# An attention and feed-forward kernel: step 3's Y transposed by DMA, the inclusive decay sums of steps 6 and 7 made by VectorE, and a new order from step 3 on

## The chip, the cores and the metric

The kernel runs on one core of one Trainium2 chip. The metric is the time of one launch on the device, in microseconds (us); lower is better. Several runs of the kernel are given by their median.

## What is computed

A linear attention with a decaying state (RWKV-6) runs over 4 sequences of 768 tokens with 8 heads of 48 channels. Its output is the input of a feed-forward layer with squared ReLU. The reference, cut to what matters:

```python
# r, k, v, w: (4, 8, 768, 48); u: (8, 48)
state = zeros((B, H, D, D))
for t in range(S):
    cur = einsum('bhd,bhe->bhde', u * k[t], v[t])
    y[t] = einsum('bhd,bhde->bhe', r[t], state + cur)
    state = w[t][..., None] * state + einsum('bhd,bhe->bhde', k[t], v[t])
# y as x: (3072, 384); w_in: (384, 2048); w_out: (2048, 384)
h = x @ w_in
out = square(maximum(h, 0)) @ w_out
```

## The kernel before

**Tiling.** The 3072 tokens are cut into 12 steps of 256 tokens, three steps for each of the four sequences. Each step has two halves of 128 tokens. A step goes through two parts. In the attention part the products of neighbouring decays are made (`ww_`), their logarithms (`lw_`), and TensorE sums those over the tokens with triangular matrices (`cum_`, lines 336 to 340): an exclusive sum, and an inclusive one with the sign turned. ScalarE takes the exponentials of both (`exp_`, `ac_`). r and k are multiplied by these decays (`rd_`), the results transposed (`tr_` and `rkt_` on TensorE and a copy, or `dtr_` by DMA), TensorE forms the products of r and k inside a chunk (`p_`, line 408), VectorE masks them (`pm_`), and the state is carried on by `su_` (TensorE, line 430), `ts_` (a sum) and `sn_` (a product on GpSimd). The output Y is collected in PSUM by `y_`, `yc_` and `yq_` (line 454); `yq_` adds the share of a token's own key through `ku_`, `qp_`, `q_` and `vq_`. `ysb_` copies Y to SBUF.

**From Y to the feed-forward part.** Y has to be transposed for the next product. `yt_` does it with six TensorE transposes into PSUM (line 500), and `xt_` copies them to SBUF. `dyt_` does it with one DMA transpose from SBUF to SBUF, issued by SP (line 507). Before, steps 0 to 3 take `yt_` and `xt_`, steps 4 to 11 take `dyt_`.

**The inclusive sum.** If a step has a word `ni_`, `cum_` leaves out its last matrix product (line 340) and VectorE makes the inclusive sum from the exclusive one and the logarithms (`ni_`, line 348). Before, steps 8 to 11 do so.

**The feed-forward part.** `m1_` makes the first product in eight groups per step (line 517, six matrix products each), `rl_` applies the ReLU (ScalarE, line 524, or VectorE, line 526), `sq_` squares (lines 532 and 534), and the second product follows as `m2_` (line 540) for steps 0 to 4. Steps 5 to 11 use Strassen's scheme in Winograd's form for it, with seven products of half size (`pw_`, line 594), sums of inputs (`sw_`, line 572, on VectorE or GpSimd) and of outputs (`cx_`, `ow_`). `store` writes the result.

**The order.** One string, `ORDER`, holds every operation of the program as a word: its name, its step, further numbers, after a colon the PSUM bank, after an equals sign the engine (A ScalarE, V VectorE, G GpSimd). The loop at the end of the kernel issues the words one after the other. Each engine therefore works through its own words in the order in which they stand in the string, and waits at a word until its inputs are there and its target is free. Loads, stores, `dtr_` and `dyt_` all go through SP's one queue in the same way. Buffers are handed out in the order of the words.

```python
    def dyt_(s):
        nc.sync.dma_start_transpose(
            out=buf("xT", s)[:].rearrange("p c a t -> p (c a) t"),
            in_=buf("y_sb", s)[:].rearrange("p c d -> p (c d)"))
    ...
        nc.tensor.matmul(cs[:, 0, 0:DM], tri_strict[:], lw[:, :, 0:D], start=True, stop=True)
        if s not in by_vector:
            nc.tensor.matmul(cs[:, 1, 0:DM], tri_incl_neg[:], lw[:, :, 0:D], start=True, stop=True)

    by_vector = {int(word.partition("=")[0].split(".")[1]) for word in ORDER.split() if word.startswith("ni_.")}
```

Of the kernel before, what the change touches and what calls it, by code (L numbers as in the profile page):

```python
# [50 lines left out]
sq_.4.1=A vq_.7 yc_.6 dtr_.7.0 yq_.6 m1_.5.4:3 ysb_.6=V lw_.8 rl_.5.5=A m1_.5.0:2 kw_.8=G ts_.7.0=V rl_.5.4=A dyt_.6
cum_.8:1 rl_.5.0=V m2_.4.1.0:0 ku_.8 ac_.8 sq_.5.3=A ni_.8=V m2_.4.0.0:1 store.3.1 rw_.8=V m1_.5.3:2 ld.8.v exp_.8
ld.9.k ww_.9=G m2_.4.0.1 sq_.5.2=A rd_.8.1 m2_.4.0.2 ld.9.r rl_.5.3=A sn_.7.0 m2_.4.0.3 rd_.8.0 ld.10.w sq_.5.1=A
m2_.4.1.1 qp_.8 ts_.7.1=V m2_.4.1.2 sq_.5.0=A p_.7.1:0 p_.7.0:1 store.3.0 os_.4.0=A pm_.7.1 sn_.7.1 m1_.6.7:2
store.0.1 m1_.6.2:3 sw_.5.1.1=G rl_.6.7=A pm_.7.0 m1_.6.6:1 rl_.6.2=A m1_.6.1:2 v_.8=A sw_.5.0.1=V sw_.5.0.2=V y_.7:1
rl_.6.6=A tw_.2=V su_.8:0 lw_.9 yc_.7 yq_.7 kw_.9=V m1_.6.3:3 ysb_.7=A rw_.9=V m1_.6.4:1 rl_.6.1=A sw_.5.0.3=V dyt_.7
sw_.5.1.3=V cum_.9:1 rl_.6.4=A ww_.10=V m2_.4.1.3 sw_.5.1.2=V rl_.6.3=A dtr_.8.0 m1_.6.5:2 ni_.9=V sq_.6.1=A tw_.4=V
pw_.5.2:1 dtr_.8.1 os_.4.1=A pw_.5.1:3 sw_.5.1.4=G exp_.9 m1_.6.0:0 cx_.5.1=V ac_.9 store.1.1 rl_.6.5=V pw_.5.6
sw_.5.0.4=G rl_.6.0=A ld.10.k rd_.9.1 m1_.7.7:2 sq_.6.0=A ld.9.v ku_.9 ow_.5.1=V m1_.7.5:0 ld.11.w rd_.9.0 rl_.7.7=A
pw_.5.5 cx_.5.2=A rl_.7.5=A ts_.8.0=V dtr_.9.0 m1_.7.4:2 lw_.10 cx_.5.3=V sn_.8.0 q_.8 p_.8.0:0 rl_.7.4=A p_.8.1:1  # L60
m1_.7.1:0 sq_.6.2=A pm_.8.0 vq_.8 pw_.5.7 rl_.7.1=A pm_.8.1 pw_.5.3 sq_.6.3=A dtr_.9.1 ku_.10 m1_.7.3:2 ow_.5.2=V
v_.9=A ow_.5.4=V m1_.7.0:0 sw_.6.1.1=V rl_.7.3=A y_.8:0 rl_.7.0=A sw_.6.1.2=V su_.9:1 sw_.6.0.1=V sq_.7.2=A yc_.8
sw_.6.0.2=V yq_.8 sw_.6.1.3=V pw_.5.4 ysb_.8=A sw_.6.0.3=V ww_.11=V m1_.7.6:1 ts_.9.0=A dyt_.8 ow_.5.3=V pw_.6.1:2
sn_.9.0 rl_.7.6=A m1_.7.2:0 sq_.7.3=A qp_.9 store.5.1 ts_.9.1=V pw_.6.2:1 ld.10.r rl_.7.2=V cx_.6.1=A lw_.11 ld.11.r
p_.9.1:0 p_.9.0:1 sq_.7.1=A ld.11.k pw_.6.6 sw_.6.1.4=G pm_.9.0 store.5.0 m1_.8.4:3 ld.10.v kw_.10=G q_.9 m1_.8.7:0
rl_.8.4=A store.4.1 cum_.10:1 cx_.6.2=A sw_.6.0.4=G ow_.6.1=V m1_.8.1:3 rl_.8.7=A ni_.10=V pw_.6.5 pm_.9.1 exp_.10
rw_.10=G pw_.6.7 rl_.8.1=A rd_.10.1 qp_.10 m1_.8.5:0 cx_.6.3=A sq_.7.0=A cum_.11:0 rd_.10.0 pw_.6.3 rl_.8.5=A
m1_.8.6:3 ni_.11=V dtr_.10.0 rw_.11=G ow_.6.2=V m1_.8.2:0 sw_.7.0.1=V rl_.8.6=A vq_.9 m1_.8.3:1 ac_.10 dtr_.10.1 q_.10
rl_.8.2=A pw_.7.1:3 exp_.11 ow_.6.4=V pw_.7.2:0 sw_.7.1.1=G cx_.7.1=A rd_.11.0 rl_.8.3=A y_.9:1 sq_.8.3=A yq_.9
ow_.7.1=V yc_.9 sw_.7.0.2=V pw_.6.4 sw_.7.0.4=V ac_.11 kw_.11=V ysb_.9=A m1_.8.0:1 sw_.7.0.3=V sw_.7.1.2=V v_.10=A  # L70
pw_.7.5 dyt_.9 rd_.11.1 sw_.7.1.4=G pw_.7.6 cx_.7.3=A ow_.6.3=A sw_.7.1.3=V rl_.8.0=A p_.10.1:1 store.6.1 ku_.11
p_.10.0:0 cx_.7.2=A pw_.7.3 dtr_.11.0 pm_.10.0 sq_.8.0=A pw_.7.7 sq_.8.2=A pm_.10.1 dtr_.11.1 m1_.9.4:2 sn_.9.1
m1_.9.0:1 sq_.8.1=A vq_.10 ow_.7.2=V store.4.0 rl_.9.4=V y_.10:1 ld.11.v su_.10:0 rl_.9.0=V m1_.9.1:2 store.7.0
ts_.10.0=V m1_.9.5:1 ow_.7.4=V rl_.9.1=A sn_.10.0 m1_.9.6:0 rl_.9.5=A qp_.11 ts_.10.1=V m1_.9.2:2 rl_.9.6=A
sw_.8.0.1=V yc_.10 p_.11.1:0 yq_.10 pw_.7.4 ysb_.10=A sw_.8.0.2=V sw_.8.1.1=V m1_.9.3:0 rl_.9.2=A pm_.11.1 dyt_.10
sw_.8.1.2=G v_.11=A m1_.9.7:1 pw_.8.1:2 q_.11 sn_.10.1 rl_.9.7=A p_.11.0:1 cx_.8.1=A ow_.7.3=V su_.11:0 rl_.9.3=A
sw_.8.1.3=V pw_.8.2:1 sq_.9.3=A pw_.8.6 ow_.8.1=V sw_.8.1.4=G pm_.11.0 m1_.10.4:0 cx_.8.2=A m1_.10.5:3 vq_.11
rl_.10.4=A ts_.11.0=V pw_.8.5 sw_.8.0.3=V rl_.10.5=A m1_.10.6:0 sq_.10.2=A sn_.11.0 sq_.9.1=V m1_.10.0:3 rl_.10.6=A
y_.11:0 rl_.10.0=A cx_.8.3=V yc_.11 sq_.9.2=V yq_.11 sw_.8.0.4=V m1_.10.7:0 ysb_.11=A sw_.9.1.1=V sq_.9.0=V pw_.8.7
rl_.10.7=A dyt_.11 sw_.9.0.1=V pw_.8.3 ow_.8.4=V m1_.10.2:0 store.7.1 ow_.8.2=V sw_.9.0.2=V pw_.8.4 rl_.10.2=V  # L80
m1_.10.3:1 sq_.10.3=V ow_.8.3=A store.8.1 m1_.11.0:2 rl_.10.3=A sw_.10.1.1=G store.6.0 m1_.11.6:0 sq_.10.1=A
rl_.11.0=V store.8.0 m1_.10.1:1 sw_.10.1.3=G rl_.11.6=V m1_.11.1:2 rl_.10.1=V m1_.11.2:0 sq_.10.0=V rl_.11.1=A
m1_.11.3:3 sw_.9.0.3=V rl_.11.2=A sw_.10.0.1=V m1_.11.5:1 sq_.11.0=A rl_.11.3=V sw_.10.0.2=G m1_.11.4:0 rl_.11.5=A
m1_.11.7:3 sw_.9.1.3=G rl_.11.4=V pw_.9.1:2 sw_.10.1.2=V sq_.11.2=A sw_.9.1.2=G pw_.9.2:1 rl_.11.7=V cx_.9.1=A
pw_.10.1:0 sq_.11.3=A pw_.10.2:3 cx_.10.1=V ow_.9.1=V sq_.11.1=A pw_.10.6 sw_.9.1.4=V sw_.9.0.4=V pw_.9.5 ow_.10.1=V
# [594 lines left out]
```

## Time and profile before

| | us |
|---|---|
| median of 3 runs | 178.15 (178.13 to 179.26) |
| profiled execution | 178.47 |
| its span | 176.7 |
| TensorE busy | 168.7 |
| VectorE busy | 141.4 |
| ScalarE busy | 135.7 |
| GpSimd busy | 125.8 |

The profiled execution is one run of its own, and its span is the part of its time that the instructions cover. In the profile PE is TensorE's matrix products, PEld its weight loads, DVE is VectorE, ACT is ScalarE, POOL is GpSimd, and SP is SyncE, whose queue issues the DMAs (SPq). A row of a group names the line, engine, operation, what is written and read, and then busy us, the mean ns of one, and the idle time just before. L517 is line 517 of the kernel. Shares of busy time are averages over stages with different limits.

### The profile page before, as it was taken

How to read it: one execution, taken by the hardware profiler on the slowest of the kernel's cores; microseconds unless marked ns; L12 is line 12 of the kernel's file. 1: busy time of each engine (PE TensorE's matmuls, PEld its weight loads, DVE VectorE, ACT ScalarE, POOL GpSimd, SP SyncE). 2: the span in 40 equal slices, each digit the busy share in tenths (PEclk: the TensorE clock that was granted, in tenths of full speed). 3: DMA queues.
4: the chain of work that ended last, by engine and by line, in shares of the span. 5: the costliest groups of instructions: out<-in, count | busy, mean ns of one | idle time of the engine just before them, and what ended most of it. 6: DMA issues, size and time to landing. Idle time of an engine off the chain costs nothing.

```text
span 176.7 us, 5829 instructions
## 1 busy us (share of the span) xinstructions
PE 168.7 (95%) x2431; PEld 133.3 (75%) x2431; DVE 141.4 (80%) x221; ACT 135.7 (77%) x229; POOL 125.8 (71%) x116
## 2 busy tenths in 40 slices
...
GB/s 142 315 305 340 380 244 347 370 347 254 152 220 240 287 199 254 184 215 179 308 225 194 329 136 222 224 113 269 251 115 132 227 53 4 108 114 4 45 93 134
DMA packets 82667, 36.55 MB, mean 207 GB/s; under 512 B 75857, under 2 KB 81106, under 8 KB 82642
## 3 DMA queue, kind: packets, MB, share of 16 engines
...
HBM read 25.17 MB, written 4.72 MB: 169 GB/s over the span
## 4 chain that ended last, share of the span: by engine, by line
PE 85%; SPq 6%; DMA 5%; issue 1%; ACT 1%; ACTq 0%
PE one L517 35%; PE one L594 19%; PE one L540 15%; PE att L454 7%; DMA w_st_b<-in_moe_w_in_dram 5%; SPq L205 4%; PE att L408 3%; PE att L430 2%; SPq L213 2%; PE att L338 1%; SPq L233 1%; PE one L500 1%; PE att L340 1%; PE one L383 1%; PE att L336 0%
## 5 line engine op out<-in xcount | busy, mean ns | idle before, releaser
L517 PE MATMUL one<-xT_b,wi_sb 128*128 128x256 bf16 x576 | 70.3, 273 | 0.6 <-ACT gt_b L524 0.4
L517 PEld LDWEIGHTS <-wi_sb 128*128 128x128 f16 x576 | 54.7, 98 | 9.4 <-issue 1.3
L524 ACT ACTIVATE gt_b<-one 128x512 f16<-128x512 f32 x70 | 40.8, 596 | 10.1 <-PE one L517 9.4
L532 ACT ACTIVATE gt_b<-gt_b 128x1024 bf16<-128x1024 f16 x42 | 43.5, 1056 | 1.4 <-DVE gt_b L526 1.0
L419 DVE TENSOR_TENSOR pmT_b<-att,mask 128x1024 bf16<-128x1024 f32 x22 | 26.3, 1217 | 4.2 <-PE att L408 4.2
L540 PE MATMUL one<-wo_sb,gt_b 128*128 128x384 f16 x160 | 28.7, 326 | 0.0
L594 PEld LDWEIGHTS <-gt_b 128*128 128x128 bf16 x280 | 23.2, 98 | 0.9 <-issue 0.4
L311 POOL TENSOR_TENSOR ku_b<-k_b,u_bc 128x768 f32<-128x768 f32 x12 | 22.3, 1862 | 1.0 <-ACT ac_buf L360 0.8
L316 POOL TENSOR_TENSOR ku_b<-ku_b,r_b 128x768 f32<-128x768 f32 x12 | 22.2, 1848 | 0.6 <-DMA r_b<-in_r_dram 0.4
L540 PEld LDWEIGHTS <-gt_b 128*128 128x128 bf16 x160 | 15.1, 98 | 9.6 <-issue 0.5
L444 POOL TENSOR_TENSOR S_b<-t_b,ac_buf 128x384 bf16<-128x384 f32 x20 | 16.9, 846 | 5.4 <-ACT t_b L438 4.8
L526 DVE TENSOR_SCALAR gt_b<-one 128x512 f16<-128x512 f32 x26 | 17.6, 686 | 3.0 <-PE one L517 2.2
L322 POOL TENSOR_TENSOR vq_b<-v_b,q_b 128x768 bf16<-128x768 f32 x12 | 18.2, 1518 | 0.9 <-DVE q_b L319 0.8
L594 PE MATMUL one<-wo_sb,gt_b 128*128 128x192 f16 x168 | 16.2, 246 | 0.0
L374 DVE TENSOR_TENSOR rdec_buf<-r_b,att 128x768 bf16<-128x768 f32 x12 | 11.4, 948 | 1.8 <-POOL r_b L304 0.8
L374 DVE TENSOR_TENSOR rdec_buf<-k_b,att 128x768 bf16<-128x768 f32 x12 | 11.4, 948 | 1.7 <-ACT ac_buf L360 1.1
L319 DVE TENSOR_REDUCE q_b<-ku_b 128x16 f32<-128x768 f32 x12 | 11.3, 944 | 1.7 <-POOL ku_b L316 1.7
L599 ACT ACTIVATE w_st_b<-one 128x192 f32<-128x192 f32 x14 | 4.4, 329 | 10.3 <-PE one L594 10.2
L304 POOL TENSOR_TENSOR r_b<-r_b,w_b 128x384 f32<-128x384 f32 x8 | 8.1, 1014 | 4.7 <-DMA r_b<-in_r_dram 4.7
L292 POOL TENSOR_TENSOR ww_b<-w_b 128x384 f32<-128x384 f32 x7 | 8.0, 1149 | 4.5 <-DMA w_b<-in_w_dram 4.5
L594 PE MATMUL one<-w_st_b,gt_b 128*128 128x192 f16 x112 | 11.2, 246 | 0.0
L440 DVE TENSOR_TENSOR t_b<-S_b,att 128x384 f32<-128x384 bf16 x16 | 8.8, 548 | 2.9 <-POOL S_b L444 2.8
...
## 6 DMA issues: line engine op xcount, KB each, us to landing
w_b<-in_w_dram SPq DMA_DIRECT2D x12, 384.0 KB, 5.9
r_b<-in_r_dram SPq DMA_DIRECT2D x12, 384.0 KB, 5.4
k_b<-in_k_dram SPq DMA_DIRECT2D x12, 384.0 KB, 5.3
v_b<-in_v_dram SPq DMA_DIRECT2D x12, 384.0 KB, 5.0
...
rkT_b<-rdec_buf SPq DMA_TRANSPOSE x18, 3.5
```

What stands on the lines that cost most here:

```text
L311: nc.gpsimd.tensor_mul(buf("ku", s)[:], buf("k", s)[:, :, 1:3, :], u_bc[:, :, None, :].to_broadcast([C, H, 2, D]))
L316: nc.gpsimd.tensor_mul(ku[:], ku[:], buf("r", s)[:, :, 0:2, :])
L322: nc.gpsimd.tensor_mul(buf("vq", s)[:].rearrange("p j h d -> p h j d"), buf("v", s)[:], buf("q", s)[:, :, :, None].to_broadcast([C, H, 2, D]))
L374: nc.vector.tensor_mul(rdec[:, i, :, heads, 0:D], x.rearrange("p h j d -> p j h d"), decay[:, None, :, :].to_broadcast([C, 2, n, D]))
L419: nc.vector.tensor_mul(pmT, ps_p[:].rearrange("p e (a x) -> p (e a) x", a=2), mk.to_broadcast([C, 4, 2 * C]))
L444: nc.gpsimd.tensor_mul(buf("S", s + c, 1 - c)[:], buf("t", s, c)[:].rearrange("p (a e d) -> p a e d", a=HP, e=2), tiles["a_c", s][:, :, c, ...
L517: nc.tensor.matmul(ps1[:, j, :], wi_sb[:, n // 4, kk, n % 4 * 128:(n % 4 + 1) * 128], xT[:, :, kk, :], start=(kk == 0), stop=(kk == KT - 1))
L524: nc.scalar.activation(rl, m1, AF.Relu, scale=RS)
L526: nc.vector.tensor_scalar(out=rl, in0=m1, scalar1=RS, scalar2=0.0, op0=ALU.mult, op1=ALU.max)
L532: nc.scalar.activation(gt, rl, AF.Square)
L540: nc.tensor.matmul(m2, gt[:, n, c * C:(c + 1) * C], wo_sb[:, n, :], start=(n == 0), stop=(n == NT - 1))
L594: nc.tensor.matmul(where_to, gt[:, n, :], wo[:, n, :], start=(n == 0 and i in (1, 2, 5)), stop=(n == NT // 2 - 1), skip_group_check=True)
```

## The change

Only the string `ORDER` is changed, from a place late in step 2's feed-forward part on. The words `yt_.3` and `xt_.3` go and `dyt_.3` comes. The words `ni_.6` and `ni_.7` come, so that `cum_.6` and `cum_.7` leave out the product of line 340. A last warm-up product (`warm_.1.5`), which stood behind all other work of TensorE, goes. All other operations stay, but from here on they stand in another order, with other banks, and many with another engine: of the Strassen combinations `sw_`, 14 go from VectorE to GpSimd and 9 the other way; of the ReLUs, 13 go from VectorE to ScalarE and 8 the other way; `rw_.5` goes from VectorE to GpSimd. The first lines, and those around steps 6 to 8 of the new order:

```diff
@@ -34,60 +34,60 @@ (inside ORDER)
-rl_.2.6=A m1_.2.3:2 sn_.3.1 rl_.2.5=A pm_.3.0 m2_.2.1.0:3 rl_.2.3=A ww_.5=G sq_.2.1=A su_.4:1 tw_.1=V y_.3:0 ld.6.r
-yc_.3 sq_.2.2=A yq_.3 m2_.2.0.0:0 rw_.5=V dtr_.4.0 lw_.5 m2_.2.1.1 tw_.3=V ysb_.3=A m2_.2.0.1 sq_.2.3=A yt_.3:2
-ts_.4.0=V cum_.5:0 kw_.5=V m2_.2.1.2 dtr_.4.1 xt_.3=V exp_.5 ww_.6=G m2_.2.1.3 rd_.5.0 sn_.4.0 m1_.3.2:1 os_.2.1=A
-rd_.5.1 m2_.2.0.2 rw_.6=G rl_.3.2=A m1_.3.6:3 lw_.6 ts_.4.1=V dtr_.5.1 v_.5=A q_.4 m1_.3.0:2 sn_.4.1 ac_.5 m1_.3.3:1
-dtr_.5.0 rl_.3.6=A ku_.5 su_.5:0 rl_.3.3=A m1_.3.4:3 ts_.5.0=V rl_.3.0=A store.1.0 m1_.3.5:1 rl_.3.4=A ld.7.w vq_.4
-p_.4.1:0 ld.6.k p_.4.0:1 pm_.4.1 m1_.3.1:3 ld.7.k sn_.5.0 m2_.2.0.3 rl_.3.1=A pm_.4.0 m1_.3.7:2 qp_.5 rl_.3.5=A
-sq_.3.0=A p_.5.1:0 y_.4:1 pm_.5.1 rl_.3.7=A yc_.4 ww_.7=G sq_.3.1=A yq_.4 m2_.3.0.0:2 ysb_.4=V ku_.6 sq_.3.2=A
-cum_.6:0 q_.5 dyt_.4 p_.5.0:1 m2_.3.1.0:1 exp_.6 kw_.6=V m2_.3.0.1 qp_.6 os_.2.0=A ac_.6 m2_.3.0.2 store.2.0 sq_.3.3=A
-rd_.6.1 ld.6.v m2_.3.1.1 ld.7.r rd_.6.0 lw_.7 m2_.3.1.2 kw_.7=G m2_.3.0.3 pm_.5.0 dtr_.6.0 vq_.5 m1_.4.1:0 q_.6
-cum_.7:0 m1_.4.0:3 ac_.7 exp_.7 y_.5:1 dtr_.6.1 rl_.4.0=V yq_.5 rl_.4.1=V yc_.5 m1_.4.7:3 os_.3.0=V ysb_.5=A rw_.7=G
...
+rl_.2.6=A m1_.2.3:2 sn_.3.1 rl_.2.5=A pm_.3.0 m2_.2.1.0:3 rl_.2.3=A rw_.5=G sq_.2.1=A su_.4:1 q_.4 y_.3:0 ww_.5=G
+yq_.3 sq_.2.2=A ts_.4.0=V yc_.3 m2_.2.0.0:0 ysb_.3=V sn_.4.0 lw_.5 m2_.2.0.1 sq_.2.3=A kw_.5=V dyt_.3 m2_.2.0.2
+ts_.4.1=V cum_.5:0 tw_.1=V m2_.2.1.1 dtr_.4.1 ac_.5 exp_.5 ww_.6=G m2_.2.1.2 dtr_.4.0 m2_.2.0.3 v_.5=A rd_.5.1 sn_.4.1
+m2_.2.1.3 rd_.5.0 vq_.4 dtr_.5.1 su_.5:1 os_.2.1=A m1_.3.4:2 tw_.3=V m1_.3.0:1 ku_.5 rl_.3.4=A dtr_.5.0 m1_.3.3:3
+ts_.5.0=V m1_.3.1:2 store.1.0 rl_.3.3=A ld.6.k rl_.3.0=A p_.4.0:0 rl_.3.1=V p_.4.1:1 ld.6.r m1_.3.6:3 pm_.4.1
+sq_.3.0=A sn_.5.0 ld.6.v m1_.3.2:1 ld.7.w qp_.5 pm_.4.0 m1_.3.7:2 os_.2.0=A rl_.3.2=A p_.5.0:1 m1_.3.5:0 rl_.3.6=A
+pm_.5.0 ld.7.k ku_.6 sq_.3.1=A y_.4:0 rl_.3.5=V yc_.4 lw_.6 yq_.4 p_.5.1:1 q_.5 rl_.3.7=A m2_.3.1.0:3 ysb_.4=A pm_.5.1
+m2_.3.0.0:1 vq_.5 sq_.3.2=A dyt_.4 m2_.3.1.1 sq_.3.3=V cum_.6:0 kw_.6=G y_.5:1 store.2.0 ni_.6=V yc_.5 ld.7.r ww_.7=V
+yq_.5 exp_.6 m2_.3.1.2 rw_.6=G store.2.1 ac_.6 ld.8.w m2_.3.0.1 ysb_.5=A rd_.6.1 m2_.3.0.2 qp_.6 v_.6=A dyt_.5 rd_.6.0
+m2_.3.0.3 lw_.7 m1_.4.2:2 kw_.7=G cum_.7:0 rl_.4.2=A su_.6:1 ni_.7=V m1_.4.3:0 os_.3.0=V exp_.7 dtr_.6.0 ts_.6.0=V
...
+sw_.5.0.3=V su_.8:0 rl_.6.1=A tw_.4=V y_.7:1 rl_.6.5=A yc_.7 yq_.7 sw_.5.1.3=V m1_.6.0:0 ysb_.7=A sw_.5.1.4=V
+sw_.5.0.2=V pw_.5.1:3 os_.4.0=A dyt_.7 sw_.5.0.4=G rl_.6.0=A cum_.9:1 cx_.5.1=V m1_.6.6:1 sq_.6.2=A ni_.9=V ld.10.k
+pw_.5.6 ku_.9 ow_.5.1=V ts_.8.0=V exp_.9 ld.10.w pw_.5.5 rl_.6.6=V ld.11.w v_.9=A p_.8.0:0 cx_.5.3=V ld.11.r m1_.7.5:0
+sq_.6.3=A pm_.8.0 m1_.7.1:1 rl_.7.5=A sw_.6.1.1=V pw_.5.3 rl_.7.1=A sw_.6.1.3=V kw_.9=V m1_.7.0:0 cx_.5.2=A sq_.6.0=A
+rd_.9.0 store.4.0 m1_.7.2:1 ku_.10 ld.10.r rd_.9.1 p_.8.1:0 rl_.7.2=A pw_.5.7 rl_.7.0=A ow_.5.2=V dtr_.9.1 m1_.7.7:1
+ww_.10=G sq_.7.0=A ow_.5.4=V sw_.6.0.1=V m1_.7.4:0 sn_.8.0 lw_.10 pm_.8.1 m1_.7.3:2 rl_.7.7=A dtr_.9.0 pw_.5.4
+ww_.11=G rl_.7.3=A sw_.6.0.2=V pw_.6.2:1 ac_.9 rl_.7.4=A sw_.6.1.2=V su_.9:0 sq_.7.1=A sw_.6.0.4=V y_.8:1 sw_.6.1.4=V
+yq_.8 sw_.6.0.3=V ts_.9.0=A yc_.8 kw_.10=V pw_.6.1:2 ow_.5.3=V ysb_.8=A sn_.9.0 sw_.7.0.1=V m1_.7.6:0 cx_.6.1=A
+rw_.10=G dyt_.8 lw_.11 ts_.9.1=V pw_.6.6 rl_.7.6=A ow_.6.1=V p_.9.0:1 qp_.10 cx_.6.2=A store.3.0 p_.9.1:0 sq_.7.3=A
...
```

More of the change, by code (lines that the diff above doesn't have):

```diff
@@ L51 @@
[L51 to L85, printed above, removed]
```

44 lines of the change are left out of this document (35 added, 9 removed).

## The prediction

> **What bounds the kernel now.** I read the busy shares first, then the busy time by stage, then the chain that ended last, and then the queues of the engines around the first place where the two orders differ. Page (busy us, share, instructions):
>
> ```profile
> PE 168.7 (95%) x2431; PEld 133.3 (75%) x2431; DVE 141.4 (80%) x221; ACT 135.7 (77%) x229; POOL 125.8 (71%) x116
> ```
>
> The stages (stretch and its length, then busy us and instructions of each engine, clock, DMA share, GB/s):
>
> ```profile
> core 0: us, PE busy (x) PEld busy (x) DVE busy (x) ACT busy (x) POOL busy (x), PEclk, DMA share, GB/s
> 22.60:48.50 25.90, 25.51 (x333) 18.28 (x332) 19.63 (x27) 22.51 (x35) 24.31 (x19) 1.00 0.97 285
> 48.50:80.00 31.50, 31.50 (x485) 23.02 (x485) 26.97 (x32) 24.13 (x43) 24.24 (x20) 1.00 1.01 229
> 80.00:120.00 40.00, 40.00 (x633) 32.73 (x631) 33.63 (x53) 37.26 (x61) 30.23 (x25) 1.00 0.99 214
> 120.00:159.70 39.70, 39.70 (x587) 35.19 (x586) 35.73 (x60) 29.73 (x53) 26.40 (x23) 1.00 0.65 137
> 159.70:173.60 13.90, 13.90 (x169) 13.69 (x166) 8.62 (x25) 5.60 (x12) 4.18 (x4) 1.00 0.17 59
> ```
>
> From 48.5 to 173.6 us TensorE has no idle time at all. Its queue runs in the order written. So only two things can change the time: the length of TensorE's own work, and new waits in its queue. Nothing that another engine gains is worth anything by itself. The chain (start, us, what) shows both prices:
>
> ```profile
> 55.63 0.45 PE att L430 x16
> 56.08 0.98 PE att L454 x44
> 57.05 2.06 PE one L540 x12
> 59.11 0.35 PE one L500 x6
> 59.46 0.08 PE att L336 x4
> 59.54 0.18 PE att L338
> 59.72 0.16 PE att L340
> ...
> 66.32 0.57 PE att L408 x32
> 66.89 0.76 PE one L517 x6
> ...
> 68.30 0.66 PE one L517 x6
> 68.96 0.35 PE att L408 x16
> 69.30 1.25 PE att L454 x52
> ...
> 159.67 13.88 PE one L594 x168
> ```
>
> The orders part just before 55.63, at the state product of step 4 (L430). What follows the last row (L594) is the drain, which both orders end in alike.
>
> **The change: TensorE's own work.** The six transposes of step 3 go (L500, 0.35). Steps 6 and 7 each lose the inclusive sum (L340, 0.16 each): 0.67 in all. The new order also changes what stands beside what. A group of six that follows attention products costs 0.76 instead of 0.66, so a return costs 0.11 (0.10 by these two rounded rows). Counting the order from there on, TensorE returns from attention products (`p_`, `su_`, `y_`, `yq_`, `yc_`) to full-width groups 20 times before and 23 times after: +0.33. A pair of `p_` side by side costs 0.57, two single ones 2 x 0.35; five pairs become six: -0.13. Sum: -0.67 + 0.33 - 0.13 = **-0.47 us**. That is all the change can bring.
>
> **The change: what is moved to others.** VectorE makes the inclusive sum of steps 6 and 7 between `cum_` and `exp_`, and no longer copies step 3's transposed Y:
>
> ```profile
> L348 DVE SCALAR_TENSOR_TENSOR att<-att,lw_buf 128x384 f32<-128x384 f32 x4 | 2.2, 560 | 0.0
> L504 DVE COPY xT_b<-one 128x768 bf16<-128x768 bf16 x4 | 2.2, 554 | 0.4 <-PE one L500 0.4
> ```
>
> Two sums add 1.12, the copy saves 0.55, and 14 Strassen combinations (`sw_`) go to GpSimd against 9 that come back: VectorE is not the engine that gets later. Each sum delays `exp_` by 0.56. Between `cum_.6` and the first product that needs it (`su_.6`) TensorE has ten groups, 5 us, against 0.56 for the sum, 0.8 for the exponential and 0.95 for the key product, so I take 0. If that cover were gone, it would cost up to 2 x 0.56.
>
> The transpose of step 3 goes to SP's queue. Its wait for `ysb_.3` holds back everything behind it: the transposes of steps 4 and 5 and the loads of step 6. Landing of such a transpose (min/median/max) and of the loads, from windows of DMA issues at 48 to 56 (r) and 56 to 70 us (k):
>
> ```profile
> DMA to landing us min/median/max: 2.5/2.7/4.1
> r_b<-in_r_dram SPq DMA_DIRECT2D x1, 384.0 KB, 6.1
> k_b<-in_k_dram SPq DMA_DIRECT2D x2, 384.0 KB, 5.4
> ```
>
> In the new order y_.3 ends at 57.05 as before and VectorE, which does `q_.4` and `ts_.4.0` first, ends `ysb_.3` at about 58.1. The transpose lands between 60.6 and 62.2. Its first reader, `m1_.3.4`, comes at about 62.6 (three groups, `cum_.5`, four groups and `su_.5` after 57.05). Cost 0, with 0.4 to 2 us to spare. On TensorE the same transpose took 0.35. The Trainium skill, "VectorE: DVE Perf Modes", section "Rules for kernel authors", says to transpose on TensorE where PSUM may be the target, and else by DMA; this speaks against the edit, but TensorE is the full engine here and the latency is covered, and by the skill's choice the sum would be 0.35 longer.
>
> **The change: new waits.** Rows of GpSimd and SP (start, us):
>
> ```profile
> 55.93 1.72 POOL L292 TENSOR_TENSOR ww_b<-w_b 128x384 f32<-128x384 f32 x1
> 61.64 1.00 POOL L292 TENSOR_TENSOR ww_b<-w_b 128x384 f32<-128x384 f32 x1 [3.98 <-DMA w_b<-in_w_dram]
> 71.86 1.83 POOL L311 TENSOR_TENSOR ku_b<-k_b,u_bc 128x768 f32<-128x768 f32 x1
> 50.64 2.53 SPq L205 DMA_DIRECT2D r_b<-in_r_dram  x1
> 58.61 6.98 SPq L391 DMA_TRANSPOSE rkT_b<-rdec_buf  x4
> 65.64 0.57 SPq L618 DMA_DIRECT2D out_dram<-w_st_b  x1
> 66.75 1.97 SPq L205 DMA_DIRECT2D k_b<-in_k_dram  x2
> L304 POOL TENSOR_TENSOR r_b<-r_b,w_b 128x384 f32<-128x384 f32 x8 | 8.1, 1014 | 4.7 <-DMA r_b<-in_r_dram 4.7
> L322 POOL TENSOR_TENSOR vq_b<-v_b,q_b 128x768 bf16<-128x768 f32 x12 | 18.2, 1518 | 0.9 <-DVE q_b L319 0.8
> L296 ACT ACTIVATE lw_buf<-ww_b 128x384 bf16<-128x384 f32 x12 | 6.2, 520 | 2.6 <-DVE ww_b L292 2.2 <-POOL ww_b L292 0.2
> ```
>
> *First wait, `cum_.5`.* `ww_.5` started on GpSimd at 55.93. Now `rw_.5`, which VectorE did, stands ahead of it there, and needs r of step 5: 50.64 + 6.1 = 56.7. So `rw_.5` ends at 57.75, `ww_.5` at 58.75 (1.00) or 59.5 (1.72), and the logarithm 0.52 later, at 59.3 to 60.0. Behind it on ScalarE stand `sq_.2.3`, `ac_.5` and `exp_.5`. TensorE reaches `cum_.5` at 59.11. Wait 0.2 to 0.9; I take 0.3 with the hand-over, since the slow 1.72 ran beside VectorE's product of r and w, which is gone there. If r landed 0.4 earlier it would be 0. `exp_.5` and the key product then end just when `su_.5` comes: 0.1 more.
>
> *Second wait, `yq_.5`.* GpSimd now does `ku_.6` ahead of `vq_.5`, and `ku_.6` needs k of step 6. SP issues that load after the transposes and a store: the last two transposes took 1.5 each before, the last would start when `rd_.5.0` ends, near 64.0, so the load goes out at about 66.2 instead of 66.75. k landed before 71.86, when `ku_.6` began without a wait: 5.1 or less, 5.4 by the window. So k is there at 71.3 to 71.6, `ku_.6` ends at 73.1 to 73.4, `vq_.5` at 74.6 to 74.9. TensorE, 0.4 late, comes to `yq_.5` at 74.3. Wait 0.3 to 0.6; I take 0.4. With a landing 1 us faster it is 0.
>
> *Third place, ScalarE in steps 6 and 7.*
>
> ```profile
> L532 ACT ACTIVATE gt_b<-gt_b 128x1024 bf16<-128x1024 f16 x42 | 43.5, 1056 | 1.4 <-DVE gt_b L526 1.0
> L524 ACT ACTIVATE gt_b<-one 128x512 f16<-128x512 f32 x70 | 40.8, 596 | 10.1 <-PE one L517 9.4
> ```
>
> Between `m1_.6.0` and `pw_.6.6` TensorE has 14.0 us of work. ScalarE must do five squares and seven ReLUs there (5 x 1.056 + 7 x 0.596 = 9.5) and ten small operations (about 4.4, from the means of their groups): 13.9, or about 1 less where neighbours overlap, after a start 0.6 late. That leaves between 0.5 short and 0.5 spare; I take 0.2. In the remaining steps I followed each engine's queue in the same way and found spares of 0.1 to 1 us, none below zero; 0, with 0 to 0.8 kept for the range.
>
> **Sum**: -0.47 + 0.3 + 0.1 + 0.4 + 0.2 = **+0.5 us**. The profiled execution took 178.47 (span 176.7 and 1.8 around it), so it would take 179.0; the median of the runs is 0.3 lower, 178.15, and gives **178.7 us**.
>
> **Rivals.**
> *None of these waits appears.* The loads land earlier than the rows bound them, TensorE stays full and only its work counts: 178.15 - 0.47 = 177.7. For it: no wait at all in 125 us before. Against: the r load's 6.1.
> *SP's queue gives a real stall (the slower side).* If the transposes behind the new one take longer, k of step 6 comes later and `yq_.5` with it. Each us that k lands after 71.0 is a us of TensorE. The four took 6.98, 1.75 each; at 2.2 each for the four plus the new one's delay, the load goes out at 68.0, k lands at 73.4, `vq_.5` ends at 76.7, wait 2.4: -0.47 + 0.3 + 0.1 + 2.4 + 0.2, about +2.5, **180.7**. It ends more than 1% up once k lands after about 72.7. For it: DMA share 1.01 there. Against: two transposes at 1.5 each at the same place.
> *GpSimd and VectorE block each other.* `ww_.5` took 1.72 against 1.00 beside VectorE's products, so something is shared. GpSimd gets five more combinations and one more of each of two products. If three of them meet a place with under 0.3 to spare and lose 0.7 each (1.72 - 1.00): +0.5 + 1.5 = 180.2. Against: VectorE's queue has less work than before. The Trainium skill, "SBUF — State Buffer", section "Who interferes with whom", has a VectorE operation with two SBUF inputs and a GpSimd operation that reads SBUF exclude each other for a whole instruction; the 1.72 agrees with it.
> *Faster by over 1%* needs 1.8 us; TensorE has 0.67 to lose and no idle time.
>
> **How the numbers follow.** Small waits 0.56 (178.7, own range 177.9 to 179.8), none 0.17, SP's queue 0.16, blocking 0.08, faster 0.03. One per cent (1.8 us) is about what a measurement can tell from no change. Within it lie the first two and half of the blocking, 0.76 with rounding; above it SP's queue, the other half and the tail of the main case, 0.21; below it 0.03. The range takes the rival without waits at its low end and the SP rival at its high end: 177.5 to 180.7.
>
> **What would show it.** TensorE: 0.2 to 0.9 idle ahead of L336 near 59 us, released by ScalarE's logarithm; 0 to 0.6 idle ahead of L454 near 74, with `vq_` as the late one and GpSimd waiting for k just before. No wait at the first `m1_.3`. L500 x18, L340 x6, L348 x6. Total TensorE idle time after 23 us of 0.6 to 2. It is wrong if the idle sum is under 0.3 or above 3, or if the main loss lies after 120 us.

## The result, and the profile after

| | before | changed |
| --- | --- | --- |
| median of the runs (us) | 178.12 (20 runs) | 179.97 (20 runs) |
| ratio | | 1.0091, 95% interval 1.0066 to 1.0116 |
| profiled execution (us) | 178.47 | 180.12 |
| its span (us) | 176.7 | 178.0 |

The forecast was 178.7 within 177.5 to 180.7. The change is slower by 0.9% by the ratio, and by 1.85 us between the medians, where 0.5 was forecast: in the range, but above the main case's own range of 177.9 to 179.8.

Busy shares of the changed kernel, and the groups that the change moves (group, count, busy us, mean ns):

```profile
PE 169.1 (95%) x2422; PEld 133.0 (75%) x2422; DVE 137.5 (77%) x213; ACT 138.9 (78%) x232; POOL 133.8 (75%) x122
```

```profile
L348 DVE SCALAR_TENSOR_TENSOR att<-att,lw_buf 128x384 f32<-128x384 f32 x6 | 3.3, 557 | 2.1 <-PE att L338 2.1
L340 PE MATMUL att<-lw_buf,tri_incl_neg 128*128 128x384 bf16 x6 | 2.1, 357 | 0.0
...
L500 PE MATMUL one<-ident,y_sb_b 128*128 128x128 bf16 x18 | 1.5, 219 | 0.5 <-ACT y_sb_b L492 0.5
```

The work has moved as announced. Now the stretch from the state product of step 4 (L430), ahead of which the orders of TensorE agree, to TensorE's last matmul: first the kernel before, then the changed one by stage (stretch and its length, TensorE's busy us, then the other engines):

```profile
55.56:173.75 118.19, 118.19 (x1766) 98.93 (x1765) 99.03 (x161) 91.63 (x159) 79.81 (x65) 1.00 0.78 173
```

```profile
54.42:70.00 15.58, 15.49 (x270) 11.08 (x270) 13.99 (x17) 11.88 (x21) 12.58 (x11) 1.00 1.10 235
70.00:80.00 10.00, 8.66 (x123) 5.90 (x122) 7.10 (x10) 6.34 (x12) 8.66 (x8) 1.00 1.19 233
80.00:130.00 50.00, 50.00 (x759) 41.62 (x758) 43.91 (x70) 46.37 (x80) 37.71 (x30) 1.00 0.94 214
130.00:140.00 10.00, 9.72 (x176) 8.29 (x175) 7.36 (x11) 8.49 (x16) 8.88 (x8) 1.00 0.82 142
140.00:150.00 10.00, 9.38 (x150) 7.60 (x151) 7.66 (x13) 8.42 (x14) 6.52 (x7) 1.00 0.27 82
150.00:174.94 24.94, 24.93 (x290) 23.89 (x290) 15.00 (x35) 13.33 (x24) 13.55 (x12) 1.00 0.19 64
```

The stretch has grown from 118.19 to 120.52 (the sum of the lengths): 2.33 more, of which 2.34 is idle time, 1.34 in one place near 77 and 0.62 in another near 143. The rest of the difference between the two profiled executions is 1.14 less ahead of this stretch (it starts at 54.42 instead of 55.56, in code that is the same), 0.12 more in the drain and 0.35 more outside the span. Where the stretch begins seems to go with the execution and not with the order: it is at 54.3 to 54.6 in ten of the fourteen traces of this document, and at 55.6 to 56.9 in the other four, the kernel before among them. Of the 1.85 between the medians some 1.5 lie inside the span, less than the 2.33 here; one trace of each kernel does not show how its waits fall in a typical run. The places, on TensorE's timeline (start, us, what, idle time before it and who ended it):

```profile
77.27 0.81 PE L517 MATMUL one<-xT_b,wi_sb 128*128 128x256 bf16 x6 [1.34 <-DMA xT_b<-y_sb_b]
...
139.91 1.47 PE L517 MATMUL one<-xT_b,wi_sb 128*128 128x256 bf16 x12 [0.24 <-DVE gt_b L526]
...
143.99 2.14 PE L517 MATMUL one<-xT_b,wi_sb 128*128 128x256 bf16 x18 [0.62 <-ACT gt_b L524]
```

At 77.27 starts `m1_.4.2`, the first reader of step 4's transposed Y: the wait is for the landing of `dyt_.4`. At 143.99 starts `m1_.10.5`, the first reader of step 10's. There the view names a ReLU, which did end at that moment:

```profile
143.40 0.60 ACT L524 ACTIVATE gt_b<-one 128x512 f16<-128x512 f32 x1 [0.22 <-PE one L517]
```

But by the order this is `rl_.9.0`, which frees bank 1, and `m1_.10.5` writes bank 3. `dyt_.10` was issued at 139.67 and landed 4.3 us later, also at 143.94. Two events end together, and the names decide which of them the matmul needs; an experiment below settles it. The windows of DMA work around the two transposes (GB/s in 40 slices, the queue of instruction fetches, and median us from issue to landing), changed kernel first:

```profile
GB/s 0 0 0 0 0 0 0 0 0 0 0 0 0 0 0 87 233 282 292 292 292 282 292 240 283 10 0 0 0 186 317 335 372 317 391 261 56 0 0 0
...
q8 instruction: 1, 0.02, 2.4%
...
xT_b<-y_sb_b SPq DMA_TRANSPOSE x1, 4.3
```

This is 139.6 to 142.9, `dyt_.10`. Its data, 768 packets of 256 bytes, move at up to 290 GB/s from 140.8 on and are through at 141.7. Just then, at 141.63 by the packets, a fetch of instructions begins: one packet of 16 KB on one of the 16 DMA engines, 1.27 us long (2.4% of 16 engines in 3.3 us). Of the 32 packets of 4 bytes that close the transpose, 30 are through by 141.72 too; the last two come at 142.89 and 142.90, just as the fetch ends, and the landing follows 1.0 later. (The flow from 142.0 on is a store behind it.) In the kernel before, step 10's transpose has its fetch ahead of its data (141.1 to 144.0):

```profile
q8 instruction: 1, 0.02, 1.9%
...
xT_b<-y_sb_b SPq DMA_TRANSPOSE x1, 2.9
```

That fetch began 0.3 us after the issue, at 141.42, when the transpose had not started to move. Step 4's transpose is the other case. SP's timeline of the changed kernel, and the DMA work from 71.1 to 77.3:

```profile
65.02 0.44 SPq L205 DMA_DIRECT2D k_b<-in_k_dram  x1
65.57 0.62 SPq L205 DMA_DIRECT2D r_b<-in_r_dram  x1
66.29 1.14 SPq L205 DMA_DIRECT2D v_b<-in_v_dram  x1
67.52 1.10 SPq L205 DMA_DIRECT2D w_b<-in_w_dram  x1
68.68 2.38 SPq L205 DMA_DIRECT2D k_b<-in_k_dram  x1
71.15 2.02 SPq L507 DMA_TRANSPOSE xT_b<-y_sb_b  x1
```

```profile
GB/s 322 330 285 144 156 119 59 129 233 275 315 327 325 327 302 274 282 249 152 43 21 19 92 195 15 0 0 0 0 2 8 10 8 10 41 354 416 377 345 322
```

Five loads stand ahead of `dyt_.4` where the order before has three. Its data begin at 73.3, behind the last load; the flow falls to 20 GB/s while one engine is still on that load, rises for a moment at 74.6, and stops: at 74.7 a fetch has begun, 1.04 us long, and some twenty packets of the transpose then under way take 1.8 us each. The transpose lands at 77.2, 6.1 us after its issue, against 2.9 for the same transpose before.

### The profile page after: what moved, and what is told of

Same layout as the page of the kernel before. It is cut to its first block, busy times and chain, and to the rows that moved or that the text cites. A ratio compares the mean times of both kernels' runs of the same rounds, so it can differ in the third digit from the quotient of the medians.

```text
span 178.0 us, 5824 instructions
## 1 busy us (share of the span) xinstructions
PE 169.1 (95%) x2422; PEld 133.0 (75%) x2422; DVE 137.5 (77%) x213; ACT 138.9 (78%) x232; POOL 133.8 (75%) x122
## 4 chain that ended last, share of the span: by engine, by line
PE 70%; DMA 13%; SPq 6%; ACT 4%; issue 2%; POOL 1%; DVE 1%; DVEq 0%; POOLq 0%; ACTq 0%
PE one L517 30%; PE one L594 18%; PE one L540 10%; DMA w_st_b<-in_moe_w_in_dram 5%; PE att L454 5%; SPq L205 4%; DMA xT_b<-y_sb_b 3%; DMA r_b<-in_r_dram 3%; PE att L408 2%; PE att L430 2%; SPq L213 1%; DMA out_dram<-w_st_b 1%; ACT gt_b L524 1%; PE att L338 1%; ACT gt_b L532 1%
## 5 line engine op out<-in xcount | busy, mean ns | idle before, releaser
L524 ACT ACTIVATE gt_b<-one 128x512 f16<-128x512 f32 x75 | 43.2, 595 | 10.6 <-PE one L517 10.1
L532 ACT ACTIVATE gt_b<-gt_b 128x1024 bf16<-128x1024 f16 x43 | 44.8, 1056 | 2.0 <-DVE gt_b L526 1.7
L444 POOL TENSOR_TENSOR S_b<-t_b,ac_buf 128x384 bf16<-128x384 f32 x20 | 17.6, 879 | 6.2 <-ACT t_b L438 4.2
L322 POOL TENSOR_TENSOR vq_b<-v_b,q_b 128x768 bf16<-128x768 f32 x12 | 18.7, 1559 | 0.5 <-DVE q_b L319 0.3
L526 DVE TENSOR_SCALAR gt_b<-one 128x512 f16<-128x512 f32 x21 | 14.4, 687 | 4.4 <-PE one L517 4.1
L594 PE MATMUL one<-wo_sb,gt_b 128*128 128x192 f16 x168 | 16.7, 246 | 0.0
L572 POOL TENSOR_TENSOR gt_b<-gt_b,w_st_b 128x512 bf16<-128x512 bf16 x7 | 7.9, 1151 | 11.0 <-PE one L594 7.0
L304 POOL TENSOR_TENSOR r_b<-r_b,w_b 128x384 f32<-128x384 f32 x9 | 9.4, 1047 | 5.3 <-DMA r_b<-in_r_dram 5.3
L353 ACT ACTIVATE att<-att 128x768 f32<-128x768 f32 x12 | 9.6, 801 | 2.1 <-DVE att L348 1.9
```

Of the source, the lines that this page charges most:

```text
L322: nc.gpsimd.tensor_mul(buf("vq", s)[:].rearrange("p j h d -> p h j d"), buf("v", s)[:], buf("q", s)[:, :, :, None].to_broadcast([C, H, 2, D]))
L444: nc.gpsimd.tensor_mul(buf("S", s + c, 1 - c)[:], buf("t", s, c)[:].rearrange("p (a e d) -> p a e d", a=HP, e=2), tiles["a_c", s][:, :, c, ...
L524: nc.scalar.activation(rl, m1, AF.Relu, scale=RS)
L526: nc.vector.tensor_scalar(out=rl, in0=m1, scalar1=RS, scalar2=0.0, op0=ALU.mult, op1=ALU.max)
L532: nc.scalar.activation(gt, rl, AF.Square)
L594: nc.tensor.matmul(where_to, gt[:, n, :], wo[:, n, :], start=(n == 0 and i in (1, 2, 5)), stop=(n == NT // 2 - 1), skip_group_check=True)
```

## The experiments

A ratio below is to the kernel before, run beside it. "Idle" is TensorE's idle time in the profiled execution from step 4's L430 on (2.34 in the changed kernel). "Room" is the time from a transpose's issue to the moment at which TensorE is ready for its first reader.

**Fetches shifted, changed kernel.** Both kernels add a loop behind the first warm-up group:

```diff
+    def tiny_(n):
+        for _ in range(n):
+            nc.tensor.matmul(one[1][:, 0:2], warm[:, 0:C], warm[:, 0:2], start=True, stop=True)
-ld.0.w warm_.10.1 ld.1.w
+ld.0.w warm_.10.1 tiny_.48 ld.1.w
```

> The changed kernel with 48 matmuls of two columns more (96 TensorE instructions with their weight loads) at the very start, where TensorE waits for the first loads anyway. They cost no time; they only shift which TensorE instruction the program's instruction fetches fall beside, by about 2.6 us at 75 us and 2 us at 142. If the two late transposes (dyt_.4 at 74 to 77, dyt_.10 at 142 to 144) are late because an instruction fetch falls into them, both waits (1.35 at m1_.4.2, 0.65 at m1_.10.5) go and the kernel takes about 178.0, 2.0 less than the changed kernel, unless a fetch now falls on another transpose without slack. If dyt_.4 is late because it stands behind five loads in SP's queue, it lands 6 us after its issue as before and the time stays at 180.0.

Measured: 183.76, ratio 1.0313 (1.0256 to 1.0369), slower by far. The edit did more than shift fetches. Rows by stretch show the granted clock (the third number from the end) below full speed from 5 to 15 us, where the changed kernel has 1.00:

```profile
5.00:10.00 5.00, 5.00 (x69) 2.64 (x67) 1.93 (x4) 3.64 (x9) 2.14 (x2) 0.84 1.15 310
10.00:15.00 5.00, 4.54 (x66) 3.31 (x69) 4.45 (x8) 3.13 (x4) 3.74 (x3) 0.82 0.95 296
```

So nothing can be concluded from its time; it is a miss of the design. The landings in its trace still tell something: `dyt_.10`, with no fetch near, took 2.5 and TensorE no longer waited at `m1_.10.5`; `dyt_.9`, met by a fetch 1.2 after its issue, took 4.7 and cost a wait of 1.69; `dyt_.4`, still behind five loads and met as well, took 6.6.

> The same with 16 small matmuls (32 TensorE instructions): the fetches come 0.9 us earlier at 75 us, at about 74.4, which is still inside the time in which dyt_.4 moves its data. By the fetch theory the wait at m1_.4.2 stays at 0.5 to 1.4 and the time between 179.0 and 180.0; by the queue theory 180.0. If this kernel gains as much as the one with 48, the shift of the fetches is not what decides.

Measured: 179.41, ratio 1.0102 (1.0035 to 1.0169). Idle 1.39. The wait at `m1_.4.2` was gone (`dyt_.4` landed after 4.3), and the one at `m1_.10.5` was 1.4: the fetch now came 1.08 behind the issue of `dyt_.10` instead of 1.96, and it landed after 4.5. The time, as expected, did not tell the theories apart; the landings did not stay where either theory had put them.

**The same in the kernel before.**

> The kernel before with 16 matmuls of two columns more at the very start, where TensorE waits for the loads. They cost no time there; all instruction fetches after come about 0.9 us earlier against the work. In the traces so far a step's transpose whose issue is followed by a fetch 1.0 to 2.1 us later lands after 4.1 to 4.7 us, and after 2.5 to 2.95 otherwise. Here the fetch at 133.47 comes to 1.5 to 1.9 us behind the issue of dyt_.9 (130.89 before, landed after 2.48), so it lands after 4.1 to 4.7; its first reader comes 3.33 after the issue, so TensorE waits 0.8 to 1.4 there: 178.9 to 179.5, about 1.0 above the kernel before. dyt_.6, hit before at 1.00 (4.11), is hit no more and lands after 2.5 to 2.9. If fetches do not matter: 178.1 and no wait.

Measured: 178.21, ratio 1.0016 (0.9991 to 1.0042): the expected wait did not come. The fetch for step 9 was still at 133.41, 2.48 behind the issue, and `dyt_.9` landed after 2.5. Others had moved by 2 to 4 us against the work: `dyt_.4` was hit now (fetch 1.9 behind its issue, landed after 4.2, with room for 4.3), `dyt_.6` was hit no longer (2.7 instead of 4.1). So a fetch cannot be put at will by adding instructions at the start; that step of my expectation was wrong. What held is the relation of a landing to the fetch that meets it.

**What a fetch does to a landing.** For that the traces of all fourteen kernels are taken together. Of the transposes of Y issued after 98 us (steps 7 to 11), where few loads are left: with a fetch that begins 1.0 to 2.1 us after the issue, 6 cases, the landing took 4.2 to 4.7 us; with one that begins 0.1 to 0.9 after it, 10 cases, 2.7 to 3.6; with none, or one at any other time, 37 cases, 2.5 to 2.6. For 16 more the traces hold no landing. A full queue does as much without a fetch near: in eight kernels of the new order the transpose of step 5, with loads and stores ahead of it on SP's queue and no fetch from 1.5 before its issue to its landing, landed after 4.2 to 5.1, and had room for more.

**One load moved behind `dyt_.4`.**

```diff
-pm_.5.0 ld.7.k ku_.6 sq_.3.1=A
+pm_.5.0 ku_.6 sq_.3.1=A
-m2_.3.0.0:1 vq_.5 sq_.3.2=A dyt_.4 m2_.3.1.1
+m2_.3.0.0:1 vq_.5 sq_.3.2=A dyt_.4 ld.7.k m2_.3.1.1
```

> The changed kernel with one load (k of step 7) issued behind the transpose dyt_.4 instead of ahead of it; everything else in place. By the queue theory dyt_.4 is issued 1.1 to 2.4 us earlier and lands before TensorE comes to m1_.4.2: 1.0 to 1.4 less, about 178.7. By the fetch theory the same here if the transpose is done before the fetch at 75.3; if its data still moves then, the wait stays, 180.0. If neither the queue nor the fetch is the cause, no change.

Measured: 179.60, ratio 1.0110 (1.0062 to 1.0158): no gain in the time. Waits of this kernel (TensorE's, total, times, longest):

```profile
PE one L517 <- DMA xT_b<-y_sb_b: 1.4, 2, 1.1
```

`dyt_.4` did its part: issued at 70.78, landed after 3.6 although a fetch came 2.9 behind the issue, and TensorE did not wait. But `dyt_.10`, hit again, landed after 4.2 with room for 3.2, and `dyt_.6` after 5.25 with room for 5.0. So the queue ahead of `dyt_.4` is a part of its lateness (6.1 became 3.6; the fetch had moved as well, so this run does not give the share of each), and taking a part of it away only shows the next waits.

**Step 3's transpose back on TensorE.**

```diff
-kw_.5=V dyt_.3 m2_.2.0.2 ts_.4.1=V cum_.5:0
+kw_.5=V yt_.3:2 m2_.2.0.2 ts_.4.1=V xt_.3=V cum_.5:0
```

> The changed kernel with Y of step 3 transposed on TensorE again and copied by VectorE, all else in the new order. TensorE works 0.35 longer. If the new transpose of step 3 on SP's queue (and the delay it gives to the four behind it and to the loads of step 6) is what makes the later waits, these go and the kernel takes 178.5 to 179.0. If the later waits have another cause, 180.3 (180.0 and 0.35), give or take what the shift of the fetches by twelve TensorE instructions does.

Measured: 179.50, ratio 1.0091 (1.0058 to 1.0125), the same ratio as the changed kernel. Idle 1.48, nearly all of it at `m1_.10.5` (landing 4.5); the wait at `m1_.4.2` was gone, as it was with 16 small matmuls and `dyt_.3` in place. So the time lies between the two expectations; the new transpose of step 3 is not what makes the wait in step 10. This kernel's time outside the span was 1.84 against 2.16 for the changed one; more on that below.

**Steps 4 and 10 transposed on TensorE.**

```diff
-sq_.3.2=A dyt_.4 m2_.3.1.1
+sq_.3.2=A m2_.3.1.1
-exp_.6 m2_.3.1.2 rw_.6=G
+exp_.6 m2_.3.1.2 yt_.4:2 rw_.6=G
-rd_.6.1 m2_.3.0.2
+rd_.6.1 xt_.4=V m2_.3.0.2
-m1_.9.6:2 v_.11=A sn_.10.1 dyt_.10
+m1_.9.6:2 yt_.10:1 xt_.10=V v_.11=A sn_.10.1
```

> The changed kernel with Y of steps 4 and 10 transposed on TensorE and copied by VectorE instead of by DMA. TensorE works 2 x 0.35 longer. If the landings of these two transposes are the waits at m1_.4.2 (1.35) and m1_.10.5 (0.65), both go: -2.0 + 0.7, about 178.7. If the waits come from the engines behind the order itself (ScalarE, VectorE), they stay and the kernel takes 180.7.

Measured: 178.39, ratio 1.0031 (1.0002 to 1.0060): 1.1 less than the changed kernel, by the ratios. The same stretch has no idle time left (0.05):

```profile
54.54:70.00 15.46, 15.46 (x270) 11.09 (x270) 13.33 (x17) 11.86 (x21) 12.87 (x11) 1.00 1.06 236
70.00:80.00 10.00, 9.95 (x137) 7.04 (x136) 8.90 (x13) 7.31 (x13) 10.00 (x8) 1.00 1.08 260
80.00:130.00 50.00, 50.00 (x760) 41.69 (x758) 43.21 (x71) 46.37 (x82) 37.01 (x31) 1.00 0.88 207
130.00:140.00 10.00, 10.00 (x184) 8.66 (x182) 7.07 (x11) 8.43 (x14) 8.56 (x8) 1.00 0.78 155
140.00:150.00 10.00, 10.00 (x170) 8.49 (x168) 9.37 (x16) 8.30 (x14) 7.17 (x7) 1.00 0.12 40
150.00:173.00 23.00, 23.00 (x260) 22.09 (x257) 14.01 (x32) 12.48 (x22) 12.03 (x11) 1.00 0.21 70
```

This settles that the two landings were the waits, the one that the view put down to ScalarE included: no engine's work ahead of them was made less, VectorE's was made more (two copies). The 0.35 of new work on TensorE would by itself cover half of the 0.62 of step 10; the next kernel removes that wait without it. This one also measures TensorE's own work: 118.41 busy, less two transposes of 0.35, is 117.71, against 118.19 before.

**Room instead of TensorE.** Three kernels leave the DMA transposes and give them time. The first finishes Y of step 10 earlier:

```diff
-yq_.10 sq_.8.0=A pw_.7.7 sn_.10.0 m1_.9.4:2 rl_.9.7=A
+yq_.10 yc_.10 rl_.9.7=A ysb_.10=A sq_.8.0=A pw_.7.7 sn_.10.0 m1_.9.4:2
-qp_.11 ts_.10.1=V yc_.10 rl_.9.4=V pw_.7.4 ysb_.10=A
+qp_.11 ts_.10.1=V rl_.9.4=V pw_.7.4
```

In this kernel and the next `yc_.10` stands ahead of `sn_.10.0`, and so multiplies the older state of the second chunk and does not wait for `sn_.10.0`. The two therefore do not compute the reference's result for step 10; number and shapes of the instructions are the same. The third keeps the right order.

> The changed kernel with Y of step 10 finished and cast earlier: the product yc_.10 right behind yq_.10, and ScalarE does rl_.9.7 and the cast ysb_.10 ahead of sq_.8.0. dyt_.10 is issued about 1.4 us earlier. By the fetch theory it then has over 4.5 us until its first reader, and the fetch at 141.6 comes behind it: it lands after 2.5 to 3 us and the wait at m1_.10.5 goes (0.65 to 1.4), 0.6 to 1.3 less than the changed kernel: 178.7 to 179.4; the wait at m1_.4.2 stays. If the wait at m1_.10.5 is for ScalarE's ReLU, as the trace names it, it stays or grows: 180.0 or more.

Measured: 179.03, ratio 1.0054 (1.0025 to 1.0082): 0.7 less than the changed kernel, as expected of the landing and not of ScalarE. `dyt_.10` landed after 2.5 with room for 4.8 and TensorE did not wait at `m1_.10.5`; the wait at `m1_.4.2` stayed (0.97).

The second adds the two moves for step 4 that the last of the three shows, and one on GpSimd:

```diff
-rw_.5=G sq_.2.1=A su_.4:1 q_.4 y_.3:0 ww_.5=G
+ww_.5=G rw_.5=G sq_.2.1=A su_.4:1 q_.4 y_.3:0
```

> The changed kernel with four moves that only give the two transposes room and undo one wait: the load k of step 7 behind dyt_.4, one product of the second layer of step 3 (m2_.3.1.3) ahead of m1_.4.2, the earlier Y of step 10, and ww_.5 ahead of rw_.5 on GpSimd. By the fetch theory all waits of over 0.3 go: 180.0 - 1.35 - 0.65 - 0.2 = 177.8, level with the kernel before or 0.3 under it. If TensorE's own work had become 0.47 shorter as forecast, 177.6 or less. If the waits are spread over the order and only move, 179 to 180.

Measured: 178.39, ratio 1.0040 (1.0010 to 1.0070). No wait for a transpose is left; `dyt_.10`, issued at 137.27, landed after 2.5 (its fetch came 3.5 behind the issue), `dyt_.4` after 3.4 with room for 5.6. Idle 0.88, in pieces of 0.2 to 0.45 for ScalarE's and VectorE's results. It is not level with the kernel before: TensorE's work is 0.32 shorter (117.87), but the idle time, 0.24 outside the span and 0.11 in the drain are more than that.

The last keeps every product of step 10 in its place:

```diff
-pm_.5.0 ld.7.k ku_.6
+pm_.5.0 ku_.6
-sq_.3.2=A dyt_.4 m2_.3.1.1
+sq_.3.2=A dyt_.4 ld.7.k m2_.3.1.1
-lw_.7 m1_.4.2:2
+lw_.7 m2_.3.1.3 m1_.4.2:2
-yq_.10 sq_.8.0=A pw_.7.7 sn_.10.0 m1_.9.4:2 rl_.9.7=A
+yq_.10 rl_.9.7=A pw_.7.7 sn_.10.0 yc_.10 ysb_.10=A sq_.8.0=A m1_.9.4:2
```

> The changed kernel with room for the two late transposes, and nothing else: the load k of step 7 behind dyt_.4 and m2_.3.1.3 ahead of m1_.4.2; for step 10, yc_.10 right behind sn_.10.0, and ScalarE does rl_.9.7 and ysb_.10 ahead of sq_.8.0. A hit transpose (4.1 to 4.7) is then covered too. The two waits and the time that TensorE loses in restarting after them go: 180.0 - 1.35 - 0.65 - 0.2 = 177.8, level with the kernel before. If the waits only move to ScalarE's and VectorE's results, 178.5 to 179.5.

Measured: 178.49, ratio 1.0053 (1.0032 to 1.0075). Both late transposes were in time (3.7 with room for 5.6; 2.5 with room for 4.1). But in the profiled execution (179.57, the slowest of its twelve) the fetch of step 6 met `dyt_.6`, which stands in a full queue:

```profile
96.66 2.58 PE L517 MATMUL one<-xT_b,wi_sb 128*128 128x256 bf16 x22 [1.22 <-DMA xT_b<-y_sb_b]
```

That transpose landed after 6.2 with room for 5.0. The time is the one expected if the waits only move. The expectation's 177.8 took the other transposes as safe; they are not.

**The two halves of the change by themselves.** The inclusive sums alone, in the order before:

```diff
-cum_.6:0 q_.5
+cum_.6:0 ni_.6=V q_.5
-cum_.7:0 ac_.7
+cum_.7:0 ni_.7=V ac_.7
```

> The kernel before with only one part of the change: the inclusive sums of steps 6 and 7 made by VectorE behind cum_.6 and cum_.7. TensorE loses 2 x 0.16 and nothing else is moved: 0.3 less, 177.8 (ratio 0.998), if VectorE's 2 x 0.56 stay covered. If they delay exp_.6 or exp_.7 to where TensorE waits for su_.6 or su_.7, 178.1 to 178.9.

Measured: 178.31, ratio 1.0018 (0.9991 to 1.0046). The 0.3 less did not show; a gain of 0.1% at most is left by the interval. In its trace TensorE's work is 0.30 shorter (117.89 against 118.19), but there is a wait of 0.45 at `yq_.5` for GpSimd's `vq_.5`. The kernel before with 16 small matmuls, which has no such sums, waits 0.57 at the same place, so the wait need not come from them. And the sums back on TensorE in the changed kernel:

```diff
-store.2.0 ni_.6=V yc_.5
+store.2.0 yc_.5
-su_.6:1 ni_.7=V m1_.4.3:0
+su_.6:1 m1_.4.3:0
```

> The changed kernel with the inclusive sums of steps 6 and 7 on TensorE again (L340 eight times). TensorE works 0.32 longer; by the sum of the prediction 180.3. If the two sums on VectorE delay exp_.6 and what follows, and with it the waits of the changed kernel, 179 or less.

Measured: 179.80, ratio 1.0136 (1.0095 to 1.0177), above the changed kernel's 1.0091 as the first expectation has it, though the intervals overlap. TensorE's busy time in the stretch was 118.45 against 118.17, 0.28 more. The trace shows nearly all of the 0.32, the times cannot.

The DMA transpose of step 3 alone, in the order before:

```diff
-sq_.2.3=A yt_.3:2 ts_.4.0=V
+sq_.2.3=A dyt_.3 ts_.4.0=V
-dtr_.4.1 xt_.3=V exp_.5
+dtr_.4.1 exp_.5
```

> The kernel before with only the other part: Y of step 3 transposed by DMA, in the old order. ysb_.3 ends at 58.9, the transpose lands after 2.5 to 4.5, at 61.4 to 63.4, and its first reader m1_.3.2 now comes at 60.7: TensorE waits 0.7 to 2.7 there and works 0.35 less, so 178.4 to 180.4. The time outside the span shows whether a ninth transpose of this kind is what raised it from 1.8 to 2.2 in the changed kernel: then 2.1 to 2.2 here, otherwise 1.8.

Measured: 182.16, ratio 1.0254 (1.0224 to 1.0283), more than the expectation's worst. SP's timeline and TensorE's:

```profile
56.75 3.28 SPq L391 DMA_TRANSPOSE rkT_b<-rdec_buf  x1
60.12 1.23 SPq L507 DMA_TRANSPOSE xT_b<-y_sb_b  x1
```

```profile
63.18 0.81 PE L517 MATMUL one<-xT_b,wi_sb 128*128 128x256 bf16 x6 [3.60 <-DMA xT_b<-y_sb_b]
```

Y was cast at 57.5, but `dtr_.4.0` stands ahead in SP's queue and held it until 60.0, which I had left out: the transpose came 2.6 late and the wait was 3.60. In the new order `dyt_.3` stands ahead of the two `dtr_.4`, and TensorE did not wait for it. The loss is larger than the wait, and the granted clock says why (rows by stretch):

```profile
60.00:64.00 4.00, 0.82 (x8) 0.68 (x7) 2.42 (x4) 0.11 (x1) 3.80 (x5) 1.00 0.99 166
64.00:68.00 4.00, 4.00 (x21) 2.65 (x20) 0.00 (x0) 2.57 (x6) 2.93 (x2) 0.57 0.95 199
68.00:72.00 4.00, 4.00 (x66) 2.97 (x65) 2.01 (x3) 2.17 (x4) 2.50 (x2) 1.00 1.01 277
```

After 3.60 us without a matmul the clock fell to half for most of the next 4 us: 0.43 of 4 us, some 1.7 us more. The Trainium skill, "TensorE: Matmul & The Clock Gate", section "What's actually happening", gives an idle window of about 3.4 us for that; the row agrees, and the waits of 1.0 to 1.4 in the other kernels cost no clock.

No kernel here beats the one before.

## Why the prediction was right or wrong

*TensorE's own work, -0.47: right in sum.* Without waits it is 117.71 against 118.19, -0.48, by the kernel with steps 4 and 10 on TensorE. In the changed kernel itself the busy time is 118.17: the 0.46 comes back with its waits. The kernels with fewer waits lie between (117.81 with one of 1.4). I had priced a wait at its idle time alone; in these traces 0 to 0.2 goes on top of each. Of the terms only L340's was taken by itself (0.28 and 0.30 of 0.32); the counts of returns and pairs were not.

*First wait, `cum_.5`, 0.3 and 0.1: the place right, the size below its range.* GpSimd and ScalarE:

```profile
55.48 1.01 POOL L304 TENSOR_TENSOR r_b<-r_b,w_b 128x384 f32<-128x384 f32 x1 [0.83 <-DMA r_b<-in_r_dram]
56.44 1.01 POOL L292 TENSOR_TENSOR ww_b<-w_b 128x384 f32<-128x384 f32 x1
```

```profile
57.48 0.52 ACT L296 ACTIVATE lw_buf<-ww_b 128x384 bf16<-128x384 f32 x1 [0.98 <-POOL ww_b L292]
```

The chain is the forecast one, `ww_.5` at 1.01 instead of 1.72 included, all 1.2 to 1.3 earlier, as the stretch itself begins 1.1 earlier; TensorE lost 0.09 there, where I had put 0.2 at the least.

*Second wait, `yq_.5`, 0.4: not there.* k of step 6 was issued at 65.02 and `ku_.6` began on GpSimd without a wait:

```profile
68.97 1.81 POOL L311 TENSOR_TENSOR ku_b<-k_b,u_bc 128x768 f32<-128x768 f32 x1
70.74 1.47 POOL L322 TENSOR_TENSOR vq_b<-v_b,q_b 128x768 bf16<-128x768 f32 x1
```

So k landed within 3.95, not 5.1 to 5.4. The 5.4 was the median of two loads in one window; in that trace k of step 6 was the first of them and took 4.55.

*ScalarE between `m1_.6.0` and `pw_.6.6`, 0.2: not there.* No idle time from 80 to 130.

*"The remaining steps: 0, with 0 to 0.8 kept": the step that failed.* I worked out the landing for the new transpose alone. For those of steps 4 to 11 I took it that they land as in the one trace before, though that trace's 2.5 to 4.1 stood in my own fence. Their rooms there are 3.0 to 5.2, and in the changed kernel 3.0 to 6.5: the change took away little room. It moved issues against fetches and put two loads more ahead of `dyt_.4`, so landings of 4.3 and 6.1 met rooms of 3.7 and 4.8. That is 1.96 of the 2.34 idle, and the main error of the sum: a term put at 0 cost 2.0. That the time still fell in the range is in part luck. Two forecast waits of 0.4 and 0.2 did not come, and the upper end of 180.7 stood there for a wait at `yq_.5` that did not come either.

*Around the span: 1.8 taken as fixed.* It is 1.77 in the median before and 2.16 after, 0.39 of the 1.85. The two kernels with one half of the change have 1.77 and 1.78, the new order with step 3 on TensorE 1.84, with steps 4 and 10 on TensorE 1.89, the other forms of the new order 2.0 to 2.2. So it is not the ninth transpose by itself; its cause stays open.

*The rivals.* The SP queue's real stall came true in its kind: a transpose or load late behind others. Its place was wrong (k of step 6 and `yq_.5` were in time), and the price was 1.3 instead of 2.4. Blocking between GpSimd and VectorE cost TensorE nothing: none of its waits ended with GpSimd, and `ww_.5` became faster. The stated signs: idle time ahead of L336 near 58, but 0.09 where 0.2 to 0.9 were given; none ahead of L454; L500 x18, L340 x6 and L348 x6; no wait at the first `m1_.3`; 2.34 of idle time in all where I gave 0.6 to 2, with 0.86 of it after 120 us.

The page that I weighed against the edit, the Trainium skill's "VectorE: DVE Perf Modes", section "Rules for kernel authors" (transpose on TensorE where PSUM may be the target), proved the better guide in two steps: TensorE there costs 0.70 and takes off 2.0 of waits. For step 3, where the landing had room (4.5 against 4.7), both ways gave 1.0091.
